# Two attention layers, twice over, on one core: values gathered through HBM, the normaliser broadcast by DMA, and a step list that sets four engines' order

## The chip, the cores and the metric

The kernel runs on one core of a Trainium2 chip. The metric is device time in microseconds (us), the median of several runs. TensorE is called PE, VectorE DVE, ScalarE ACT, GpSimd POOL, and SyncE, whose queue issues most DMAs, SP.

## The reference, cut to what matters

There are 2048 tokens of width 512, 32 heads of 16. Two kinds of layer alternate, A B A B, each on the layer norm of x and added to x:

```
# A: linear attention; pq = q @ w_phi, pk = k @ w_phi, per head
phi = concat(softmax(p), softmax(-p))            # 32 features
kv = phi_k^T v (16 columns); z = sum over tokens of phi_k
o = (phi_q @ kv) / (phi_q . z + 1e-6);  x += o @ wo
# B: each token attends to itself and the tokens 2, 4, ... 14 before it
logits[w] = q . k[s - 2w] / 4 (w = 0..7), masked where s < 2w
o = sum over w of softmax(logits)[w] * v[s - 2w];  x += o @ wo
```

All arrays are bf16. In A, `kv` and `z` sum over all tokens, so every block of tokens of an A layer must be through its keys before any block can go on. In B a block needs only the last 14 tokens of the block before it.

## The kernel before, in words

Tokens are worked in 4 blocks (b = 0 to 3) of 512. L is 0 or 1, the first or second pair of layers. Each block goes through these stages, generator functions in the code:

- `g_ln_first` (layer norm of the input) and, later, the end of `g_out`: ACT and DVE make `rstd`, DVE writes the normalised `xn` (L184), SP transposes it by DMA into `xnT` (L187).
- `g_fold`: at the start w_phi is multiplied into the q and k weights (`WA`), through `wraw`, the loaded raw weights, and `wT`.
- `g_a1`: keys and values of A (L263, L271), exponentials `Ek` on ACT, the softmax sums and scaling on DVE (L282 to L290), and the products summed into three PSUM banks (L296).
- `g_a2`: queries of A (L311), `Eq` on ACT, sums `rS` (L322).
- `g_akv`: once all four blocks are summed, the state goes to SBUF as `ZM` and `R` (L341, L348). This is the barrier of an A layer.
- `g_a3`: denominators (L359), the normaliser `rho` (L374) with time and head on partitions; PE spreads `rho` over the 128 feature rows by 32 matmuls with the 0/1 matrix `indB` (L381) and DVE multiplies that PSUM result into `Eq`, 8 times 128x512 (L386).
- `g_a4`: L397, then `g_out`: 16 matmuls with the output weights (L222), DVE adds to x and sums the rows (L228; L225 in the last layer), one `nmean` (L237), squares on ACT (L242).
- `g_b1`: q, k, v of B, 48 matmuls (L417) and 12 copies by ACT (L419). `QT`, and `KV[0]`, `KV[1]` with 16 columns of the block before (L421). Partition p holds head and one of four parts of the head's 16 dimensions; the 4 column groups c hold the rest.
- `g_b2`: four times, one DVE product `prod` of q with the 8 shifted keys, 128x4096 (L438), and 8 matmuls that sum the dimensions, each with a 128x32 stationary matrix in one of four column positions of the array (L443). Softmax on ACT (L449 to L461) and DVE gives `PT`, whose partitions hold offset and head. Eight DMAs copy it to `Pbc` (L472), where each partition has the weights of its head for all 8 offsets.
- `g_b3`: four times, one DVE product `pav` of `Pbc` with the 8 shifted values (L485), and 8 matmuls with the 128x128 identity that add the offsets (L489); ACT copies to `oT` (L491). Then `g_out`.

`load_B` loads the B weights (`wbraw`, L153; `WoB`, L159) and has POOL reorder them into `WB`; `weight_bound` and `flag` check a bound on the data (a slower path would run otherwise; it does not).

The order of PE, DVE and ACT is that in which the program issues its instructions. `run` gives each generator a start time and conditions, each `yield` returns a number of us, and `drain` always advances the generator with the least time. SP and POOL are not in `_ORDERED`, so their order is the scheduler's. Each engine takes its instructions strictly in its order. Tiles come from rings: 6 buffers of 8 KB a partition (`big`: `Ek`, `prod`, `pav`, `Pbc`), 18 of 4 KB (`med`), 7 of `t2`, 8 PSUM banks.

Of the kernel before, what the change touches and what calls it, by code (L numbers as in the profile page):

```python
# [16 lines left out]
P = 128  # L17
# [12 lines left out]
KVW = 16 + TB  # L30
COLN2_MAX = 3.0
# [4 lines left out]
_ORDERED = {mybir.EngineType.PE, mybir.EngineType.DVE, mybir.EngineType.Activation}  # L36


class _Fast:

    def __init__(self, ctx, tc, A_x, A_wqkv, A_w_phi, A_wo, B_wqkv, B_wo, out):
        self.tc, self.nc = tc, tc.nc
        self.out = out
        e = ctx.enter_context
        self.const = e(tc.tile_pool(name="const", bufs=1))
        self.bigp = e(tc.tile_pool(name="bigp", bufs=6))
        self.medp = e(tc.tile_pool(name="medp", bufs=18))
        self.t2p = e(tc.tile_pool(name="t2p", bufs=7))
        self.small = e(tc.tile_pool(name="small", bufs=2))
        self.psp = e(tc.tile_pool(name="psp", bufs=8, space=PSUM))  # L50
        self.A_x, self.A_wqkv, self.A_w_phi, self.A_wo = A_x, A_wqkv, A_w_phi, A_wo
        self.B_wqkv, self.B_wo = B_wqkv, B_wo

# [11 lines left out]


    def constants(self):
        nc, const = self.nc, self.const
        nc.scalar.preload_act_table_set("natural_log_exp_and_others")
# [9 lines left out]
        with nc.allow_low_precision(reason="0/1 masks"):  # L79
# [5 lines left out]
            maskQ = const.tile([P, H], BF16, name="maskQ")  # L85
            nc.vector.tensor_reduce(out=maskQ[:], in_=ident[:].rearrange("p (h k) -> p h k", k=4),
                                    axis=AX.X, op=ALU.add)
            mask32 = const.tile([P, H], BF16, name="mask32")
            nc.vector.tensor_reduce(out=mask32[:], in_=ident[:].rearrange("p (k h) -> p h k", h=H),
                                    axis=AX.X, op=ALU.add)  # L90
        self.indQK = maskQ
# [24 lines left out]
        nc.gpsimd.memset(self.ones[:], 1.0)  # L116


    def setup(self):
        nc, const = self.nc, self.const  # L120
        self.WA = const.tile([P, NB, 3 * D], BF16, name="WA")
# [20 lines left out]
        PHI = self.t2([NB, DH, 8], "PHI")  # L142
        nc.vector.tensor_tensor(
            out=PHI[:], in0=phis[:].unsqueeze(3).to_broadcast([P, NB, DH, 8]),
            in1=self.maskH[:].unsqueeze(1).unsqueeze(1).to_broadcast([P, NB, DH, 8]), op=ALU.mult)
        self.PHI, self.wraw = PHI, wraw

    def load_B(self):
        nc = self.nc
        wbraw = [self.med([NB, D], "wbraw%d" % i) for i in range(3)]  # L150
        wbv = self.B_wqkv.rearrange("(m p) c -> p m c", p=P)
        for i in range(3):
            nc.sync.dma_start(out=wbraw[i][:], in_=wbv[:, :, i * D:(i + 1) * D])  # L153
        wo_v = self.B_wo.rearrange("(h c dl) n -> dl h c n", c=NB, dl=4)
        for dl in range(4):
            d0 = self.WoB[dl:dl + 1, :, :]
            ps_ = self.WoB[:].ap[0][0]
            dst = bass.AP(d0.tensor, d0.offset, [[4 * ps_, H], [D, NB], [1, D]])
            nc.sync.dma_start(out=dst, in_=wo_v[dl])  # L159
        for i in range(3):  # L160
            for m in range(NB):
                nc.gpsimd.tensor_copy(
                    out=self.WB[:, m, i, :, :].rearrange("p c (h dl) -> p c h dl", dl=4),
                    in_=wbraw[i][:, m, :].rearrange("p (h c dl) -> p c h dl", c=NB, dl=4))

    def weight_bound(self):
        nc = self.nc
        for qk in range(2):
            sq = self.med([NB, D], "sq")
            w = self.WA[:, :, qk * D:(qk + 1) * D]  # L170
            nc.gpsimd.tensor_tensor(out=sq[:], in0=w, in1=w, op=ALU.mult)
            pn = self.ps()
            for m in range(NB):
                nc.tensor.matmul(pn[:], lhsT=self.ones[:], rhs=sq[:, m, :], start=(m == 0), stop=(m == NB - 1))
            okm = self.t2([D], "okm")
            nc.vector.tensor_scalar(out=okm[:], in0=pn[:], scalar1=COLN2_MAX, scalar2=None,
                                    op0=ALU.is_le, op1=ALU.add, accum_out=self.okc[:, qk:qk + 1])


    def ln_apply(self, key, b, mean, rstd, op0):  # L180
        nc = self.nc
        xn = self.med([4, D], "xn")
        for t in range(4):
            nc.vector.tensor_scalar(out=xn[:, t, :], in0=self.x[b][:, t, :], scalar1=mean[:, t:t + 1],  # L184
                                    scalar2=rstd[:, t:t + 1], op0=op0, op1=ALU.mult)
        xnT = self.med([4, NB, P], "xnT")
        nc.sync.dma_start_transpose(out=xnT[:].rearrange("k t c p -> k (t c) p"),  # L187
                                    in_=xn[:].rearrange("p t d -> p (t d)"))
        self.xnT[key, b] = xnT

    def rstd_of(self, var, scale):
        nc = self.nc
        lnv = self.small.tile([P, 4], F32, name="lnv", tag="lnv")
        nc.scalar.activation(out=lnv[:], in_=var, func=ACT.Ln, bias=self.eps_t[:, 0:1], scale=scale)
        rstd = self.small.tile([P, 4], F32, name="rstd", tag="rstd")
        nc.scalar.activation(out=rstd[:], in_=lnv[:], func=ACT.Exp, scale=-0.5)
        return rstd

    def g_ln_first(self, b):
        nc = self.nc  # L200
        stat = self.small.tile([P, 4, 6], F32, name="stat", tag="stat")
        mv = self.small.tile([P, 4, 2], F32, name="mv", tag="mv")
        mean = self.small.tile([P, 4], F32, name="mean", tag="mean")
        for t in range(4):
            nc.vector.bn_stats(out=stat[:, t, :], in_=self.x[b][:, t, :])
            nc.vector.bn_aggr(out=mv[:, t, :], in_=stat[:, t, :])
            if t == 1:
                yield 2.0
        nc.vector.tensor_copy(out=mean[:], in_=mv[:, :, 0])
        rstd = self.rstd_of(mv[:, :, 1], 1.0)  # L210
        yield 2.0
        self.ln_apply("A0", b, mean, rstd, ALU.subtract)

    def g_out(self, key, b, Wo, last, dt):
        nc = self.nc
        xb = self.x[b]
        oT = self.oT[key, b]
        sums = None if last else self.small.tile([P, 4], F32, name="sums", tag="sums")
        for t in range(4):
            y = self.ps()  # L220
            for c in range(NB):
                nc.tensor.matmul(y[:], lhsT=oT[:, c, t * P:(t + 1) * P], rhs=Wo[:, c, :],  # L222
                                 start=(c == 0), stop=(c == NB - 1))
            if last:
                nc.vector.scalar_tensor_tensor(out=xb[:, t, :], in0=y[:], scalar=1.0, in1=xb[:, t, :],  # L225
                                               op0=ALU.mult, op1=ALU.add)
            else:
                nc.vector.scalar_tensor_tensor(out=xb[:, t, :], in0=y[:], scalar=1.0, in1=xb[:, t, :],  # L228
                                               op0=ALU.mult, op1=ALU.add, accum_out=sums[:, t:t + 1])
            if t < 3:  # L230
                yield dt
        if last:
            ov = self.out.rearrange("b (j p) d -> p (b j) d", p=P)
            nc.sync.dma_start(out=ov[:, 4 * b:4 * b + 4, :], in_=xb[:])
            return
        nmean = self.small.tile([P, 4], F32, name="nmean", tag="nmean")
        nc.vector.tensor_scalar(out=nmean[:], in0=sums[:], scalar1=-1.0 / D, scalar2=None, op0=ALU.mult)  # L237
        yield 0.8
        ss = self.small.tile([P, 4], F32, name="ss", tag="ss")
        sqd = self.t2([D], "sqd")  # L240
        for t in range(4):
            nc.scalar.activation(out=sqd[:], in_=xb[:, t, :], func=ACT.Square, bias=nmean[:, t:t + 1],  # L242
                                 accum_out=ss[:, t:t + 1])
        rstd = self.rstd_of(ss[:], 1.0 / D)
        yield 3.5
        self.ln_apply(key, b, nmean, rstd, ALU.add)
# [984 lines left out]
```

## Time and profile before

| | |
|---|---|
| median of 3 runs (lowest, highest) | 517.25 us (516.18, 518.67) |
| the profiled execution | 517.38 us, span 515.6 us |
| PE busy | 401.8 us, 78% |
| DVE busy | 326.1 us, 63% |
| ACT busy | 262.7 us, 51% |
| granted TensorE clock, mean | 0.892 |
| moved by DMA | 25.70 MB |

The span runs from the first to the last instruction of the profiled execution; the run's own time is 1.8 us longer. Busy time of PE counts overlapping matmuls once.

### The profile page before, as it was taken

What the parts mean: (1) busy time and instruction counts of PE and PEld (TensorE: products, weight loads), DVE (VectorE), ACT (ScalarE), POOL (GpSimd) and SP (SyncE); (2) the same over time, 40 slices, a digit from 0 to 9 for tenths busy, and PEclk for the clock granted to TensorE, in tenths of its full rate; (3) what the DMA queues carried; (4) which work ended last, traced back from release to release, by engine and by line L of the source; (5) the groups of instructions that cost most, each with busy time, mean ns of one, the idle gap of its engine ahead of it and who ended that gap; (6) DMA issues with size and microseconds to landing.
All of it is one profiled execution on the core that took longest, in us unless ns stands there. A gap on an engine that the chain in (4) does not pass through costs nothing.

```text
span 515.6 us, 6841 instructions
## 1 busy us (share of the span) xinstructions
PE 401.8 (78%) x2713; PEld 180.2 (35%) x2713; DVE 326.1 (63%) x482; ACT 262.7 (51%) x559; POOL 22.0 (4%) x40
## 2 busy tenths in 40 slices
PE   2769789469967899699689679665896699996493
PEld 1435444224412343244234335422342234342141
DVE  6972234664694896839757524346469389698683
ACT  2566568144844663665546478425374556361210
POOL 2004900000000000000000000000000000000000
PEclk9888889778979899899799969868896879999987
DMA  8726000002202530320320040000131053040402
GB/s 273 178 41 165 0 1 0 3 0 42 42 4 38 123 74 9 69 54 2 61 62 1 0 83 1 0 1 10 32 43 30 12 122 74 9 120 18 108 1 88
DMA packets 51559, 25.70 MB, mean 50 GB/s; under 512 B 35136, under 2 KB 51520, under 8 KB 51520
## 3 DMA queue, kind: packets, MB, share of 16 engines
q1 hardware_dynamic: 49936, 24.12, 20.4%
q10 hardware_dynamic: 1584, 1.07, 0.7%
q8 instruction: 23, 0.38, 0.3%
q14 instruction: 16, 0.13, 0.1%
HBM read 6.31 MB, written 2.10 MB: 16 GB/s over the span
## 4 chain that ended last, share of the span: by engine, by line
PE 53%; DVE 26%; ACT 10%; DMA 5%; issue 3%; SPq 2%; DVEq 0%; ACTq 0%
PE ps L417 14%; PE ps L489 8%; PE ps L222 7%; PE ps L263 5%; DVE Eq L386 5%; DVE prod L438 5%; PE ps L271 5%; ACT sqd L242 4%; PE ps L296 4%; DVE Ek L290 4%; PE ps L311 3%; DVE x L228 3%; PE ps L397 3%; DVE pav L485 3%; DMA xnT<-xn 2%
## 5 line engine op out<-in xcount | busy, mean ns | idle before, releaser
L417 PE MATMUL ps<-xnT,WB 128*128 128x512 bf16 x384 | 101.3, 400 | 3.2 <-DMA xnT<-xn 2.7
L485 DVE TENSOR_TENSOR pav<-Pbc,KV 128x4096 bf16<-128x4096 bf16 x32 | 72.3, 2287 | 10.6 <-DMA Pbc<-PT 10.2
L489 PE MATMUL ps<-pav,ident 128*128 128x512 bf16 x256 | 64.8, 401 | 10.2 <-DVE pav L485 10.2
L438 DVE TENSOR_TENSOR prod<-QT,KV 128x4096 bf16<-128x4096 bf16 x32 | 72.7, 2286 | 0.0
L228 DVE SCALAR_TENSOR_TENSOR x<-ps,x 128x512 bf16<-128x512 f32 x48 | 32.7, 689 | 52.6 <-PE ps L222 52.6
L417 PEld LDWEIGHTS <-WB 128*128 128x128 bf16 x384 | 36.6, 101 | 57.3 <-issue 18.9
L419 ACT CAST KV<-ps 128x512 bf16<-128x512 f32 x64 | 37.0, 593 | 24.2 <-PE ps L417 24.2
L242 ACT ACTIVATE sqd<-x,nmean 128x512 bf16<-128x512 bf16 x48 | 34.7, 722 | 28.5 <-DVE nmean L237 27.4
L491 ACT CAST oT<-ps 128x512 bf16<-128x512 f32 x32 | 18.8, 586 | 48.0 <-PE ps L489 48.0
L263 PE MATMUL ps<-WA,xnT 128*128 128x512 bf16 x128 | 36.9, 435 | 8.0 <-DMA xnT<-xn 8.0
L489 PEld LDWEIGHTS <-ident 128*128 128x128 bf16 x256 | 26.1, 103 | 46.5 <-issue 17.3
L397 PE MATMUL ps<-Eq,R 128*128 128x512 bf16 x64 | 25.4, 535 | 21.4 <-DVE Eq L386 20.2
L386 DVE TENSOR_TENSOR Eq<-ps,Eq 128x512 bf16<-128x512 f32 x64 | 39.4, 683 | 1.8 <-PE ps L381 1.6
L315 ACT ACTIVATE Eq<-ps 128x512 bf16<-128x512 f32 x64 | 34.6, 594 | 8.2 <-PE ps L311 8.2
L282 DVE TENSOR_TENSOR s<-Ek 128x2048 bf16<-128x2048 bf16 x8 | 9.8, 1226 | 43.9 <-ACT Ek L266 43.9
L419 ACT CAST QT<-ps 128x512 bf16<-128x512 f32 x32 | 18.5, 585 | 35.2 <-PE ps L417 35.2
L222 PEld LDWEIGHTS <-oT 128*128 128x128 bf16 x256 | 24.5, 100 | 33.6 <-issue 5.8
L222 PE MATMUL ps<-WoA,oT 128*128 128x512 bf16 x128 | 33.9, 396 | 0.1
L311 PE MATMUL ps<-xnT,WA 128*128 128x512 bf16 x128 | 32.0, 379 | 0.0
L271 PE MATMUL ps<-WA,xnT 128*128 128x512 bf16 x128 | 31.7, 379 | 0.0
L222 PE MATMUL ps<-WoB,oT 128*128 128x512 bf16 x128 | 31.6, 379 | 0.0
L290 DVE TENSOR_TENSOR Ek<-Ek,rk 128x4096 bf16<-128x4096 bf16 x8 | 18.6, 2327 | 19.3 <-ACT rk L288 19.3
(102 smaller groups left out, 436.8 us busy)
## 6 DMA issues: line engine op xcount, KB each, us to landing
Pbc<-PT SPq DMA_DIRECT2D x64, 128.0 KB, 2.7
x<-in_A_x_dram SPq DMA_DIRECT2D x4, 512.0 KB, 9.7
out_dram<-x SPq DMA_DIRECT2D x4, 512.0 KB, 3.0
wbraw<-in_B_wqkv_dram SPq DMA_DIRECT2D x3, 512.0 KB, 5.6
wraw<-in_A_wqkv_dram SPq DMA_DIRECT2D x1, 512.0 KB, 4.3
WA<-in_A_wqkv_dram ACTq DMA_DIRECT2D x1, 512.0 KB, 7.5
wraw<-in_A_wqkv_dram ACTq DMA_DIRECT2D x1, 512.0 KB, 10.0
WoA<-in_A_wo_dram SPq DMA_DIRECT2D x1, 512.0 KB, 10.4
```

Source lines behind the costliest of these rows:

```text
L222: nc.tensor.matmul(y[:], lhsT=oT[:, c, t * P:(t + 1) * P], rhs=Wo[:, c, :], start=(c == 0), stop=(c == NB - 1))
L228: nc.vector.scalar_tensor_tensor(out=xb[:, t, :], in0=y[:], scalar=1.0, in1=xb[:, t, :], op0=ALU.mult, op1=ALU.add, accum_out=sums[:, t:t ...
L242: nc.scalar.activation(out=sqd[:], in_=xb[:, t, :], func=ACT.Square, bias=nmean[:, t:t + 1], accum_out=ss[:, t:t + 1])
L263: nc.tensor.matmul(pk[:], lhsT=xnT[:, t, k, :], rhs=WA[:, k, D:2 * D], start=(k == 0), stop=(k == NB - 1))
L271: nc.tensor.matmul(pv[:], lhsT=xnT[:, t, k, :], rhs=WA[:, k, 2 * D:3 * D], start=(k == 0), stop=(k == NB - 1))
L311: nc.tensor.matmul(pq[:], lhsT=WA[:, k, hb * P:(hb + 1) * P], rhs=xnT[:, :, k, :], start=(k == 0), stop=(k == NB - 1))
L386: nc.vector.tensor_tensor(out=ev, in0=pb[t][:].rearrange("p (a i) -> p a i", a=NB), in1=ev, op=ALU.mult)
L417: nc.tensor.matmul(pp[:], lhsT=WB[:, k, i, c, :], rhs=xnT[:, :, k, :], start=(k == 0), stop=(k == NB - 1))
L419: nc.scalar.copy(out=QT[:, c, :] if i == 0 else KV[i - 1][:, c, 16:KVW], in_=pp[:])
L438: nc.vector.tensor_tensor(out=prod[:], in0=QT[:, c:c + 1, :].to_broadcast([P, NW, TB]), in1=self.win(KV, 0, c), op=ALU.mult)
L485: nc.vector.tensor_tensor(out=pav[:], in0=Pbc[:], in1=self.win(KV, 1, c), op=ALU.mult)
L489: nc.tensor.matmul(po[:], lhsT=self.ident[:], rhs=pavs[c - 1][:, w, :], start=(w == 0), stop=(w == NW - 1))
```

## The change

It rewrites the stages as lists of steps (`step(stage, engine, function)`), and a table of 1387 entries says which step is issued next. The table now sets SP's order too. What the steps do is mostly what they did. These parts differ:

- **Values of B.** `KV[1]` goes. ACT writes `V`, SP writes it to HBM (`VD`, rows of 16 + 2048 tokens, the first 16 zero), and eight DMAs read it back as two `Vg` tiles per block, with key offset and head on the partitions and the 16 dimensions of the head one after the other along the row. Partition group g of four holds the values shifted by 2g tokens, and a window 8 tokens further along the same rows gives the other four offsets. `Pbc` and its 64 DMAs go: `pav` multiplies `PT` itself, broadcast along the dimension, with `Vg`.
- **Sum over offsets.** Eight matmuls per `pav` with the 128x32 matrix `indAV` in four column positions, in place of eight with the 128x128 identity.
- **Normaliser of A.** For blocks 1, 2 and 3, `rho` is written to HBM (`RD`) and read back spread over 128 partitions (`Prho`), in two halves; DVE multiplies each half in one 128x2048 operation. Block 0 keeps the matmuls.
- **Layer norm.** `nmean` is made per 128 tokens: four DVE operations of 128x1 for one of 128x4.
- **Loads.** The loads of the B weights stand ahead of the first transposes. `WoB` has another row order. The output is stored in halves.
- **Buffers.** `big` 8, `med` 16, `t2` 6.
- **Order.** `a2` of blocks 1 and 2 of the first pair, and the weight bound, stand behind the first barrier instead of ahead of it.

The diff, cut to its core (line numbers named in the prediction for the changed kernel are its own):

```diff
-_ORDERED = {mybir.EngineType.PE, mybir.EngineType.DVE, mybir.EngineType.Activation}
+_OPT = {"rho_dma": (1, 2, 3), "pe_resid": {}}
+_ORDERED = {_E.PE, _E.DVE, _E.Activation, _E.SP}
+_ORDER = """
+i i i f i c i g i 0 c i 3 i f e i 3 3 h f j j 3 j f f 3 h 0 f j 4 0 j h j 3 3 j 3 j 3 0 j 5 j 0 1 6 j 0 j 0 0
...
-        self.bigp = e(tc.tile_pool(name="bigp", bufs=6))
-        self.medp = e(tc.tile_pool(name="medp", bufs=18))
-        self.t2p = e(tc.tile_pool(name="t2p", bufs=7))
+        self.bigp = e(tc.tile_pool(name="bigp", bufs=8))
+        self.medp = e(tc.tile_pool(name="medp", bufs=16))
+        self.t2p = e(tc.tile_pool(name="t2p", bufs=6))
...
+        def mean(t):
...
+            nc.vector.tensor_scalar(out=T["nm"][:, t:t + 1], in0=T["sums"][:, t:t + 1], scalar1=-1.0 / D,
+                                    scalar2=None, op0=ALU.mult)
...
+        def wr(s):
...
+            a = rd[0:1, s, 0:1, :]
+            dst = bass.AP(a.tensor, a.offset, [[P, 16], [2 * 16 * P, 8], [1, P]])
+            nc.sync.dma_start(out=dst, in_=T["rho"][:, s, :])
+        def rdb(s):
...
+            src = bass.AP(a.tensor, a.offset, [[0, 16], [2 * 16 * P, 8], [1, 16 * P]])
+            nc.sync.dma_start(out=pr[:].rearrange("p t a i -> p (t a i)"), in_=src)
+        def muld(s):
+            ev = self.Eq[L, b][s]
+            nc.vector.tensor_tensor(out=ev[:], in0=ev[:], in1=T["P", s][:], op=ALU.mult)
...
-        Pbc = self.big([NW, TB], "Pbc")
...
-                nc.sync.dma_start(out=Pbc[:, hf * 4 + g, :], in_=src)
...
+        def vwr():
+            nc.sync.dma_start(out=vd[:, :, 16 + b * TB:16 + (b + 1) * TB], in_=T["V"][:])
+        def vrd(hd, g):
...
+            v0 = vd[0:1, 0:1, b * TB + 2:b * TB + 3]
+            src = bass.AP(v0.tensor, v0.offset + 2 * g + hd * 8 * ROW, [[16 * ROW, H], [ROW, 8], [1, VGW]])
+            nc.sync.dma_start(out=self.Vg[L, b][hd][32 * g:32 * g + 32, :, :], in_=src)
...
-                nc.vector.tensor_tensor(out=pav[:], in0=Pbc[:], in1=self.win(KV, 1, c), op=ALU.mult)
...
-                    nc.tensor.matmul(po[:], lhsT=self.ident[:], rhs=pavs[c - 1][:, w, :],
-                                     start=(w == 0), stop=(w == NW - 1))
...
+        def pav(q):
...
+            a = Vg[q // 2][:, (q % 2) * 4:(q % 2) * 4 + 4, 0:TB]
+            vw = bass.AP(a.tensor, a.offset, [list(a.ap[0]), list(a.ap[1]), [8, 2], [1, TB]])
+            nc.vector.tensor_tensor(out=pv[:], in0=PT[:].unsqueeze(1).to_broadcast([P, NB, 2, TB]), in1=vw,
+                                    op=ALU.mult)
+        def mo(q):
...
+            for hf in range(2):
+                for c in range(NB):
+                    nc.tensor.matmul(po[32 * c:32 * c + 32, :], lhsT=self.indAV[:], rhs=T["p", q][:, c, hf, :],
+                                     start=(hf == 0), stop=(hf == 1), tile_position=(0, 32 * c))
...
-        self.drain()
+        for w in _ORDER.split():
+            key = self.names[int(w, 36)]
+            i = n.get(key, 0)
+            n[key] = i + 1
+            self.threads[key][i]()
```

More of the change, by code (lines that the diff above doesn't have):

```diff
@@ L293, in g_a1, with kv @@
+        def kv(t):
+            if L not in self.kvp:
+                self.kvp[L] = [self.ps() for _ in range(3)]
             for s in range(2):
@@ L337, in bank, with z @@
             return n, self.kvp[L][i][:, 0:n * (P + 1)].rearrange("p (r c) -> p r c", c=P + 1)
[L339 removed]
+        def z(i):
             n, kv = bank(i)
```

888 lines of the change are left out of this document (520 added, 368 removed).

## Prediction

> **What bounds the kernel now.** I read the page's head and chain first, then busy time by stretches cut at the two barriers.
>
> ```profile
> span 515.6 us, 6841 instructions
> PE 401.8 (78%) x2713; PEld 180.2 (35%) x2713; DVE 326.1 (63%) x482; ACT 262.7 (51%) x559; POOL 22.0 (4%) x40
> PE 53%; DVE 26%; ACT 10%; DMA 5%; issue 3%; SPq 2%; DVEq 0%; ACTq 0%
> ```
>
> PE holds over half of the chain, yet is idle for 113.8 us; no engine is full. The tile view of `ZM` gives the barriers: it is first written at 92.8 us and last at 332.9. In the stretches the columns are the stretch, its length, then busy us (instructions) of PE, PEld, DVE, ACT, POOL, then the granted clock, DMA share, GB/s.
>
> ```profile
> L341 DVE TENSOR_TENSOR ZM<-ps,maskR x6: 175/182/184, 92.8 to 332.9; 128x24 bf16<-128x24 f32 x4, 128x16 bf16<-128x16 f32 x2
> 0.00:92.80 92.80, 68.83 (x518) 39.38 (x519) 47.30 (x97) 54.28 (x111) 21.02 (x34) 0.91 0.34 91
> 92.80:332.90 240.10, 194.62 (x1329) 85.23 (x1327) 152.62 (x219) 135.50 (x292) 0.98 (x6) 0.89 0.17 36
> 332.90:515.60 182.70, 138.39 (x874) 55.54 (x873) 126.22 (x167) 72.89 (x156) 0.00 (x0) 0.88 0.21 47
> 0.00:19.70 19.70, 6.75 (x60) 5.88 (x61) 14.70 (x46) 5.40 (x10) 2.87 (x17) 0.97 0.91 267
> 92.80:121.80 29.00, 17.11 (x202) 7.43 (x200) 17.60 (x42) 9.87 (x22) 0.00 (x0) 0.71 0.10 19
> 290.00:300.00 10.00, 1.96 (x9) 0.63 (x8) 3.38 (x11) 6.87 (x18) 0.00 (x0) 0.75 0.28 52
> 332.90:363.50 30.60, 16.04 (x197) 7.10 (x196) 18.64 (x44) 9.59 (x22) 0.00 (x0) 0.77 0.10 18
> 363.50:475.00 111.50, 98.22 (x574) 38.47 (x578) 82.94 (x99) 55.93 (x119) 0.00 (x0) 0.91 0.23 48
> 475.00:515.60 40.60, 24.13 (x107) 9.97 (x99) 24.64 (x25) 7.37 (x15) 0.00 (x0) 0.89 0.23 67
> ```
>
> The first two parts go by PE (68.8 of 92.8 us, 194.6 of 240.1). The last is mixed: after each barrier both PE and DVE wait (16.0 and 18.6 busy of 30.6), in the middle PE is full (98.2 of 111.5), at the end neither is (24 of 41). So I sum the three parts separately, by PE twice and then by the engine that becomes the fuller one.
>
> **Part by part.** The rows that price the edits, from the groups by line (busy us, mean ns | idle before):
>
> ```profile
> L489 PE MATMUL ps<-pav,ident 128*128 128x512 bf16 x256 | 64.8, 401 | 10.2 <-DVE pav L485 10.2
> L443 PE MATMUL ps<-prod,maskQ 128*32 128x512 bf16 x256 | 20.5, 399 | 4.8 <-DVE prod L438 4.8
> L381 PE MATMUL ps<-rho,indB 32*128 32x128 bf16 x256 | 7.8, 228 | 10.2 <-DVE rho L374 7.3 <-DVE Eq L386 2.7 <-DVE x L228 0.2
> L386 DVE TENSOR_TENSOR Eq<-ps,Eq 128x512 bf16<-128x512 f32 x64 | 39.4, 683 | 1.8 <-PE ps L381 1.6
> L282 DVE TENSOR_TENSOR s<-Ek 128x2048 bf16<-128x2048 bf16 x8 | 9.8, 1226 | 43.9 <-ACT Ek L266 43.9
> L485 DVE TENSOR_TENSOR pav<-Pbc,KV 128x4096 bf16<-128x4096 bf16 x32 | 72.3, 2287 | 10.6 <-DMA Pbc<-PT 10.2 <-issue 0.4
> L237 DVE TENSOR_SCALAR nmean<-sums 128x4 f32<-128x4 f32 x12 | 2.0, 171 | 0.4
> L421 DVE COPY KV<-KV 128x64 bf16<-128x64 bf16 x12 | 2.1, 176 | 0.0
> L311 PE MATMUL ps<-xnT,WA 128*128 128x512 bf16 x128 | 32.0, 379 | 0.0
> L322 PE MATMUL ps<-Eq,indS 128*32 128x128 bf16 x256 | 7.5, 228 | 8.1 <-ACT Eq L315 7.7
> L174 PE MATMUL ps<-sq,ones 128*128 128x512 bf16 x8 | 1.9, 379 | 0.0
> ```
>
> *Sum over offsets.* The new 256 matmuls have the form, count and column positions of L443: 20.5 us for L489's 64.8, so PE loses 44.3 us, 22.15 in each of the last two parts. (The Trainium skill, TensorEngine Tiling (Array Packing), Theoretical Speedup and Key Properties, states up to 4x for four column tiles, but that a change of tiling mode drains the array. By 4x alone the new matmuls would take 16.2 us and the total would be 4 us lower; L443 shows 3.2x, the shortfall in line with such a drain, so the row stands.)
>
> *Normaliser.* Three blocks of four lose L381 (7.8 x 3/4 = 5.9 us of PE) and L386 (39.4 x 3/4 = 29.6 us of DVE). They gain 12 products of 128x2048, priced by L282 at 1.23 us: 14.7. DVE gains 14.8 us, 7.4 a half.
>
> *Products of B.* `pav` keeps its elements and types; I keep 2287 ns. *Small ones.* 36 more `nmean` at 0.17 cost DVE 6.1 us, 4.1 and 2.1 by halves; half of L421 goes, 0.5 us each. ACT's 262.7 us do not change.
>
> *What is moved out of the first part.* `a2` of two blocks (32.0/8 + 7.5/8 = 4.94 us of PE each) and L174 (1.9): 11.8 us of PE pass behind the barrier. ACT at the first barrier, before:
>
> ```order
> L327 ACTIVATE rS<-ps 128x256
> L328 ACTIVATE rS<-rS 128x256
> L370 ACTIVATE Ds<-Ds,deneps_t 128x128
> L371 ACTIVATE Ds<-Ds 128x128
> L399 CAST oT<-ps 128x512 x4
> ```
>
> and now, where L589 and L590 are those denominators and L512 the exponentials of `a2`:
>
> ```order
> L589 ACTIVATE Ds_963<-Ds_963,deneps_t_99 128x128
> L590 ACTIVATE Ds_963<-Ds_963 128x128
> L589 ACTIVATE Ds_974<-Ds_974,deneps_t_99 128x128
> L590 ACTIVATE Ds_974<-Ds_974 128x128
> L512 ACTIVATE Eq_987<-ps_967 128x4x128
> L512 ACTIVATE Eq_988<-ps_967 128x4x128
> L512 ACTIVATE Eq_987<-ps_980 128x4x128
> L512 ACTIVATE Eq_988<-ps_980 128x4x128
> L512 ACTIVATE Eq_987<-ps_992 128x4x128
> ```
>
> Two blocks' denominators stand together now, and projections fill the time in which PE waited for DVE's products.
>
> *The start.* SP before, and now below it:
>
> ```order
> L138 DMA x_86<-in_A_x_dram 128x4x512
> L139 DMA WoA<-in_A_wo_dram 128x4x512
> L159 DMA WoB<-in_B_wo_dram 32x4x512 x4
> L187 DMA_TRANSPOSE xnT<-xn 128x16x128 x4
> L153 DMA wbraw_674<-in_B_wqkv_dram 128x4x512
> ```
>
> ```order
> L206 DMA x_89<-in_A_x_dram 128x4x512
> L207 DMA WoA<-in_A_wo_dram 128x4x512
> L257 DMA wbraw<-in_B_wqkv_dram 128x4x512 x3
> L266 DMA WoB<-in_B_wo_dram 32x2048 x4
> L269 DMA vd_146<-zpad 512x1x16
> L322 DMA_TRANSPOSE xnT<-xn 128x16x128 x4
> ```
>
> Three loads of 512 KB have passed ahead of the transposes, for whose results the first projections wait.
>
> ```profile
> wbraw<-in_B_wqkv_dram SPq DMA_DIRECT2D x3, 512.0 KB, 5.6
> 19.74 1.91 PE L263 MATMUL ps<-WA,xnT 128*128 128x512 bf16 x4
> ```
>
> 1.57 MB at the 267 GB/s of the first 19.7 us are 5.9 us, so projections start at 25.6, not 19.7. Bounds: 0 (if the queue has room) and 9 (half of three loads at 5.6 us each).
>
> *First part:* 68.8 - 6.75 = 62.1 us of PE lay behind 19.7, less 11.8 is 50.3. Idle there was 11.0; I keep 7. 25.6 + 50.3 + 7 = **83** (79 to 89).
>
> *Second part:* 194.6 - 22.15 - 2.9 + 11.8 = 181.3 us of PE. Of its idle 45.5 us, the moved `a2` fills about 10 of the 11.9 behind the barrier and 5 of the 10.2 behind `Pbc` go. In 290:300, where PE waited for the last block's layer norm, most of 8.0 goes: keys, values and sums of other blocks now stand there. That leaves 22; I take 20. **201** (189 to 221). DVE's 152.6 - 7.4 + 4.1 - 0.5 = 148.8 and ACT's 145.8 fit under it. (The Trainium skill, TensorE: Matmul & The Clock Gate, Part 1, states that PE's clock halves after an idle window of about 3.4 us and recovers after a busy one. The 0.71 granted in 92.8:121.8 agrees. If the filled gap brought full clock there, 17.1 x 0.29 = 5 us more would go, which the sum above does not take.)
>
> *Third part:* PE falls to 138.4 - 22.15 - 2.9 = 113.3, DVE to 126.2 - 7.4 + 2.1 - 0.5 = 120.4: DVE becomes the fuller engine. It was idle 12.0 us after the barrier, 28.6 in the middle, 16.0 at the end. After the barrier the DMA path adds a write and a read, partly beside block 0's matmuls: 15 (12 to 24). In the middle PE no longer holds it: 9 (4 to 18). At the end the wait for `Pbc` (4.9 us of 10.2) goes and a shorter sum follows: 8. 120.4 + 15 + 9 + 8 = **152** (140 to 172).
>
> *The gather.* DVE's b2 and b3 of the first pair, before:
>
> ```order
> L465 TENSOR_TENSOR PT_1815<-E_1784,rden_1799 128x1024
> L421 COPY KV_1582<-KV_1331 128x4x16
> L438 TENSOR_TENSOR prod_1853<-QT_1580,KV_1581 128x4096
> L438 TENSOR_TENSOR prod_1870<-QT_1580,KV_1581 128x4096
> L438 TENSOR_TENSOR prod_1886<-QT_1580,KV_1581 128x4096
> L438 TENSOR_TENSOR prod_1908<-QT_1580,KV_1581 128x4096
> L485 TENSOR_TENSOR pav_1936<-Pbc_1817,KV_1331 128x4096
> ```
>
> and now:
>
> ```order
> L769 TENSOR_TENSOR PT_1948<-E_1838,rden_1934 128x1024
> L794 TENSOR_TENSOR pav_1950<-PT_1948,Vg_1773 128x4096
> L794 TENSOR_TENSOR pav_1964<-PT_1948,Vg_1773 128x4096
> L794 TENSOR_TENSOR pav_1978<-PT_1948,Vg_1804 128x4096
> L794 TENSOR_TENSOR pav_1998<-PT_1948,Vg_1804 128x4096
> ```
>
> Before, another block's four products had to hide the copy of `PT`; now `pav` follows `PT` at once, and what it needs from DMA depends on the value projection alone. But that is more:
>
> ```profile
> Pbc<-PT SPq DMA_DIRECT2D x64, 128.0 KB, 2.7
> out_dram<-x SPq DMA_DIRECT2D x4, 512.0 KB, 3.0
> WoB<-in_B_wo_dram SPq DMA_DIRECT2D x4, 128.0 KB, 7.5
> 170.00:180.00 10.00, 10.00 (x53) 3.82 (x52) 8.80 (x8) 6.10 (x11) 0.17 (x1) 0.90 0.72 159
> ```
>
> A gather is 32 x 8 x 520 x 2 B = 266 KB, eight a block 2.13 MB, four blocks 8.5 MB in each half. At the 267 GB/s of the start's loads that is 8 us a block, at the 159 GB/s of a burst of `Pbc` 13; the write of V, priced by the output's 512 KB, 3.0. Eight `prod` of two blocks (8 x 2.29 = 18 us) stand ahead of the first `pav`, and one block's `pav` (9) ahead of the next's, so I cost the gathers at nothing; without that cover a block would pay 11 to 16 us.
>
> *SP's written order.* Twice as many bytes now share one queue whose order nobody else mends: in the second part 16 gathers stand ahead of the transpose of the last block to leave A, and in the third the stores, which wait for DVE, stand among the last 16 gathers.
>
> ```profile
> L472 SPq DMA_DIRECT2D Pbc<-PT x64: 543/604/994, 172.6 to 485.0; - x64
> DMA to landing us min/median/max: 4.2/4.3/6.2
> ```
>
> The trace has no gather. By a `Pbc` issue (0.6 us) 16 take 10 us; by a gather's bytes at 159 GB/s, 27. The transpose (4.3 us to landing, second row) is then late by up to that, and behind it stand that block's q, k and v. PE has other blocks' projections and sums meanwhile; I take 0 and let the upper bounds of the second and third part carry 10 each.
>
> **Sum.** 83 + 201 + 152 = 436 us of span, plus 1.8 (517.38 less 515.6) = **438**. The median of 517.25 is within 0.2 of the profiled execution, so the sum is compared with it directly.
>
> **The rivals.** *Only the work goes.* The new order merely moves the waits: PE's 401.8 - 44.3 - 5.9 = 351.6, the old idle 113.8 less the 10.2 behind `Pbc`, plus 5.9 at the start: 461, run **463**. For it: waits for PE by DVE and ACT are spread over many groups. Against: 20 us of the idle time lie in two stretches (92.8:121.8 and 290:300) that get other work. 0.18.
>
> *Nearly gapless.* The low ends, 79 + 189 + 140 + 1.8 = **410**. For it: 363.5:475 shows PE 88% busy already. Against: barrier and layer norm chains stay. 0.15.
>
> *Slower: the gather sets the pace.* From barrier to V's write 50 us (30.6 and 20 of projections), then 8.5 MB at r, then a block's products and the end, 20: 70 + 8500/r. At the 70 GB/s of four `WoB` loads in flight (0.52 MB in 7.5 us) the last part takes 191 and the second some 243: 83 + 243 + 191 + 1.8 = **519**. It decides below 70 GB/s; the burst rows show twice that. 0.05.
>
> That the column tiles do not overlap, so that the change does not do what it says, L443 excludes.
>
> **The numbers.** The forecast, 420 to 455, has 0.60; the remaining 0.02 is a tie. I predict 438. The range 404 to 466 takes in the forecast, most of the next two cases, and leaves the slower one out. A measurement of this kernel can tell about 0.5% from no change: faster 0.93, same 0.02, slower 0.05.
>
> **What would show it.** Right: the group of `indAV` near 20 us; `Eq` by `Prho` near 1.23 us each; the barrier at 79 to 89 and the second 189 to 221 later; no wait of `pav` for `Vg` over a few us; DVE fuller than PE in the last part. Wrong: `pav` waiting for `Vg` by the ten us, `Eq` for `Prho` beyond 15 us after a barrier, or SP holding transposes behind gathers.

## The result and the profile after

The changed kernel takes **424.23 us** (median of 4 runs, 423.0 to 424.97); the kernel before, beside it, 516.81 (516.18 to 518.67). The ratio is 0.820, 95% interval 0.817 to 0.823: 18% faster, and 14 us below the 438 forecast. The profiled run took 424.97, of which 422.1 is span; the 2.9 around it were 1.8 before.

The busy times of the page, and its chain:

```profile
PE 327.1 (78%) x2499; PEld 147.4 (35%) x2521; DVE 317.0 (75%) x476; ACT 253.6 (60%) x559; POOL 18.1 (4%) x39
PE 41%; DMA 24%; DVE 19%; ACT 10%; issue 2%; SPq 1%; ACTq 0%; DVEq 0%
```

PE is as full as before in share (78%), DVE is nearly as full (75%, from 63%), and waits for DMA hold 24% of the chain, up from 5%. The tile view of `ZM` and the busy time between the barriers (columns as before):

```profile
L547 DVE TENSOR_TENSOR ZM<-ps,maskR x6: 175/183/184, 74.5 to 268.0; 128x24 bf16<-128x24 f32 x4, 128x16 bf16<-128x16 f32 x2
0.00:74.50 74.50, 50.24 (x378) 29.11 (x383) 48.85 (x93) 42.72 (x89) 17.11 (x33) 0.93 0.47 114
74.50:268.00 193.50, 167.34 (x1357) 75.40 (x1369) 148.70 (x226) 139.97 (x314) 0.83 (x5) 0.94 0.48 95
268.00:422.10 154.10, 109.51 (x772) 42.87 (x777) 119.44 (x158) 70.92 (x156) 0.15 (x1) 0.85 0.54 119
74.50:114.00 39.50, 35.87 (x398) 16.98 (x398) 30.21 (x83) 32.17 (x78) 0.15 (x1) 1.00 0.45 98
```

The parts take 74.5, 193.5 and 154.1 us, for 92.8, 240.1 and 182.7 before and 83, 201 and 152 forecast. The stretch behind the first barrier (last row) is the plainest sign of the new order: PE was busy 17 of 29 us there, at a granted clock of 0.71; now it is busy 36 of 39.5, at 1.00.

The groups that answer to the rows that priced the edits:

```profile
L801 PE MATMUL ps<-pav,indAV 128*32 128x512 bf16 x256 | 22.6, 449 | 23.9 <-DVE pav L794 23.5 <-ACT oT L807 0.3
L627 DVE TENSOR_TENSOR Eq<-Eq,Prho 128x2048 bf16<-128x2048 bf16 x12 | 14.6, 1222 | 11.2 <-DMA Prho<-rd 11.2
L794 DVE TENSOR_TENSOR pav<-PT,Vg 128x4096 bf16<-128x4096 bf16 x32 | 71.9, 2287 | 17.7 <-DMA Vg<-vd 8.9 <-PE ps L801 8.6
L382 DVE TENSOR_SCALAR nmean<-sums 128x1 f32<-128x1 f32 x48 | 7.2, 153 | 1.4
L676 PE MATMUL ps<-xnT,WB 128*128 128x512 bf16 x384 | 87.6, 384 | 4.2 <-DMA xnT<-xn 4.1
```

Every edited operation costs what its nearest row said, within about 2 us in each group. The projections of B (L676) were not edited and still show 87.6 us of busy time, for 101.3 before; this comes up again below. The idle times behind the bar have changed: `pav` waits 17.7 us (10.6 before), `Eq` 11.2 for `Prho`, and PE waits longer for the transposed input `xnT`. The page's rows of that wait are below, the changed kernel's and then those of the kernel before, with the landing of the transposes after the change:

```profile
L506 PE MATMUL ps<-xnT,WA 128*128 128x512 bf16 x128 | 31.9, 400 | 13.8 <-DMA xnT<-xn 13.2
L435 PE MATMUL ps<-WA,xnT 128*128 128x512 bf16 x123 | 30.4, 391 | 9.8 <-DMA xnT<-xn 9.4
DMA to landing us min/median/max: 4.2/4.7/10.0
```

```profile
L263 PE MATMUL ps<-WA,xnT 128*128 128x512 bf16 x128 | 36.9, 435 | 8.0 <-DMA xnT<-xn 8.0
L417 PE MATMUL ps<-xnT,WB 128*128 128x512 bf16 x384 | 101.3, 400 | 3.2 <-DMA xnT<-xn 2.7
```

With the 4.1 of L676 that is 26.7 us for 10.7. Of the 26.7, 9.4 lie at the start and 17.3 in the second part, where the kernel before waited 8.0 in one place. The 13.2 are one wait, at 185 to 198 us: 14 gathers are issued from 176 to 187, and the transpose behind them, of the first block to leave B, takes 10.0 us to land. The 7.3 us that `pav` waits for sums in the second part lie there too, since PE, which makes the sums, stands at that transpose.

The DMA issues of the page, with the median from issue to landing at the end of a row:

```profile
Vg<-vd SPq DMA_DIRECT2D x64, 260.0 KB, 8.1
vd<-V SPq DMA_DIRECT2D x8, 512.0 KB, 3.3
```

### The profile page after: what moved, and what is told of

Read it like the earlier page. It is cut to its first block, busy times and chain, and to the rows that moved or that the text cites. A ratio compares the mean times of both kernels' runs of the same rounds, so it can differ in the third digit from the quotient of the medians.

```text
span 422.1 us, 6496 instructions
## 1 busy us (share of the span) xinstructions
PE 327.1 (78%) x2499; PEld 147.4 (35%) x2521; DVE 317.0 (75%) x476; ACT 253.6 (60%) x559; POOL 18.1 (4%) x39
## 4 chain that ended last, share of the span: by engine, by line
PE 41%; DMA 24%; DVE 19%; ACT 10%; issue 2%; SPq 1%; ACTq 0%; DVEq 0%
PE ps L676 16%; DMA xnT<-xn 5%; PE ps L506 5%; PE ps L363 5%; PE ps L423 4%; DMA vd<-V 4%; DMA Prho<-rd 4%; DMA Vg<-vd 3%; DMA rd<-rho 3%; DVE x L376 3%; PE ps L478 3%; DVE xn L317 3%; ACT Eq L512 2%; DMA wraw<-in_A_wqkv_dram 2%; PE ps L435 2%
## 5 line engine op out<-in xcount | busy, mean ns | idle before, releaser
L676 PE MATMUL ps<-xnT,WB 128*128 128x512 bf16 x384 | 87.6, 384 | 4.2 <-DMA xnT<-xn 4.1
L794 DVE TENSOR_TENSOR pav<-PT,Vg 128x4096 bf16<-128x4096 bf16 x32 | 71.9, 2287 | 17.7 <-DMA Vg<-vd 8.9
L734 DVE TENSOR_TENSOR prod<-QT,K 128x4096 bf16<-128x4096 bf16 x32 | 71.4, 2285 | 3.1 <-ACT QT L690 1.6
L676 PEld LDWEIGHTS <-WB 128*128 128x128 bf16 x384 | 37.0, 99 | 53.6 <-issue 10.5
L376 DVE SCALAR_TENSOR_TENSOR x<-ps,x 128x512 bf16<-128x512 f32 x64 | 42.9, 684 | 10.6 <-PE ps L363 10.5
L506 PE MATMUL ps<-xnT,WA 128*128 128x512 bf16 x128 | 31.9, 400 | 13.8 <-DMA xnT<-xn 13.2
L807 ACT CAST oT<-ps 128x512 bf16<-128x512 f32 x32 | 18.4, 590 | 40.2 <-PE ps L801 40.2
L512 ACT ACTIVATE Eq<-ps 128x512 bf16<-128x512 f32 x64 | 34.0, 625 | 13.4 <-PE ps L506 13.4
L801 PE MATMUL ps<-pav,indAV 128*32 128x512 bf16 x256 | 22.6, 449 | 23.9 <-DVE pav L794 23.5
L435 PE MATMUL ps<-WA,xnT 128*128 128x512 bf16 x123 | 30.4, 391 | 9.8 <-DMA xnT<-xn 9.4
L429 ACT ACTIVATE Ek<-ps 128x512 bf16<-128x512 f32 x64 | 32.9, 636 | 2.6 <-PE ps L423 2.6
L363 PE MATMUL ps<-WoB,oT 128*128 128x512 bf16 x124 | 32.6, 408 | 1.1 <-ACT oT L807 0.8
L423 PE MATMUL ps<-WA,xnT 128*128 128x512 bf16 x122 | 29.0, 379 | 0.7 <-DVE WA L241 0.4
L690 ACT CAST QT<-ps 128x512 bf16<-128x512 f32 x32 | 18.7, 586 | 13.4 <-PE ps L676 13.4
L658 ACT CAST oT<-ps 128x512 bf16<-128x512 f32 x32 | 16.8, 597 | 14.1 <-PE ps L652 14.1
L506 PEld LDWEIGHTS <-WA 128*128 128x128 bf16 x128 | 12.8, 102 | 30.9 <-DMA xnT<-xn 13.8
L627 DVE TENSOR_TENSOR Eq<-Eq,Prho 128x2048 bf16<-128x2048 bf16 x12 | 14.6, 1222 | 11.2 <-DMA Prho<-rd 11.2
```

Source lines behind the costliest of these rows:

```text
L376: nc.vector.scalar_tensor_tensor(out=xb[:, t, :], in0=T[t][:], scalar=1.0, in1=xb[:, t, :], op0=ALU.mult, op1=ALU.add, **kw)
L423: nc.tensor.matmul(pk[:], lhsT=xnT[:, t, k, :], rhs=self.WA[:, k, D:2 * D], start=(k == 0), stop=(k == NB - 1))
L429: nc.scalar.activation(out=T["E"][:, t, s, :], in_=T["k", t][:], func=ACT.Exp, scale=1.0 - 2.0 * s)
L435: nc.tensor.matmul(pv[:], lhsT=xnT[:, t, k, :], rhs=self.WA[:, k, 2 * D:3 * D], start=(k == 0), stop=(k == NB - 1))
L506: nc.tensor.matmul(pq[:], lhsT=self.WA[:, k, hb * P:(hb + 1) * P], rhs=xnT[:, :, k, :], start=(k == 0), stop=(k == NB - 1))
L512: nc.scalar.activation(out=self.Eq[L, b][s][:, :, hb, :], in_=T[hb][:].rearrange("p (t i) -> p t i", t=4), func=ACT.Exp, scale=1.0 - 2.0 * s)
```

## The experiments

My theory from the two traces: (a) the operations take off what the rows say, but most of the gain comes from the list that fills PE's gaps; (b) what is left is held by transfers, for the bytes of the gathers delay the transposes in the second part and the last products in the third. The rivals: the operations alone do it; the gathers are hidden as forecast; the start is held by the loads ahead of the transposes. All times below are medians of four runs unless said otherwise, beside 424.2.

**The operations without the list.** The kernel before with the new operations, its planner and the order of its loads kept. Its gathers stand where the copies of `PT` stood, behind the softmax.

```diff
-                nc.vector.tensor_tensor(out=pav[:], in0=Pbc[:], in1=self.win(KV, 1, c), op=ALU.mult)
...
+                nc.vector.tensor_tensor(out=pav[:], in0=PT[:].unsqueeze(1).to_broadcast([P, NB, 2, TB]), in1=vw,
+                                        op=ALU.mult)
...
+                for hf in range(2):
+                    for k in range(NB):
+                        nc.tensor.matmul(po[32 * k:32 * k + 32, :], lhsT=self.indAV[:], rhs=pavs[c - 1][:, k, hf, :],
```

> The kernel before with the new operations (V written and gathered through HBM, column-tiled sums, the normaliser of blocks 1 to 3 by DMA, the new WoB layout, buffers 8/16/6) but with the old planner and its start times; loads and nmean as before. Theory, operations and order each carry a part: 450 to 475 us, PE busy near 352 us, PE idle still over 100 us. Rival one, the operations carry it all: 424 to 435 us. Rival two, the list alone carries it: over 500 us.

Measured **494.58 us**, ratio 0.954 (0.948 to 0.961). Its stretches, and its 384 projections of B:

```profile
0.00:93.60 93.60, 68.62 (x512) 39.27 (x520) 47.35 (x98) 54.53 (x111) 20.87 (x34) 0.91 0.35 91
93.60:323.80 230.20, 175.67 (x1219) 70.95 (x1233) 145.32 (x198) 133.73 (x292) 0.83 (x5) 0.87 0.38 80
323.80:493.50 169.70, 116.08 (x769) 42.31 (x777) 118.64 (x146) 71.95 (x156) 0.00 (x0) 0.85 0.50 108
L441 PE MATMUL ps<-xnT,WB 128*128 128x512 bf16 x384 | 103.3, 406 | 0.6 <-DMA xnT<-xn 0.6
L422 PE MATMUL ps<-Eq,R 128*128 128x512 bf16 x64 | 24.5, 510 | 32.6 <-DVE Eq L399 24.5 <-DVE Eq L411 8.1
```

That is between the 450 to 475 of the theory and the second rival's 500. The operations alone give 4.6 of the 18.0 per cent; the list, with the loads and the split mean that go with it, gives the other 13.4 on top of them. The list with the old operations was not run, so the split holds in this order alone. PE loses 41 us of busy time (401.8 to 68.6 + 175.7 + 116.1 = 360.4), but the run only 23, since PE now waits longer elsewhere (32.6 us for `Eq` in front of L422, where the same products, L397, waited 21.4 before). The sum is also a warning about busy time: the same matmuls as in the changed kernel are busy 360.4 us here and 327.1 there.

**The sum over offsets undone, one pair at a time.** Each `pav` is summed by eight matmuls of full width, the selector padded with zeros, for the eight that share the columns.

```diff
+                        nc.tensor.matmul(po[:], lhsT=self.indW[:, (3 - c) * H:(7 - c) * H], rhs=T["p", q][:, c, hf, :],
+                                         start=(hf == 0 and c == 0), stop=(hf == 1 and c == NB - 1))
```

In the first pair:

> The changed kernel, but in the first pair of layers the sum over offsets is made by eight full 128x128 matmuls with zero-padded matrices instead of four column positions: 22 us more PE work between the barriers, same result. Theory, PE bounds the second part (167 of 193.5 us busy): 439 to 446 us. Rival, PE's idle time there absorbs it: 424 to 431 us.

In the second pair:

> The same in the second pair of layers alone: 22 us more PE work behind the second barrier. Theory, DVE and the gathers set the last part (PE 109.5 of 154.1 us busy): 427 to 436 us, under half of the added work. Rival, PE is on the path there too: 442 to 447 us.

Measured **433.73** and **428.61 us**. The part that the edit touches, of each:

```profile
75.20:277.80 202.60, 185.83 (x1354) 85.73 (x1368) 149.22 (x226) 140.90 (x314) 0.83 (x5) 0.97 0.45 91
```

```profile
268.00:426.50 158.50, 126.41 (x770) 53.42 (x777) 119.55 (x158) 71.08 (x156) 0.15 (x1) 0.91 0.53 116
```

PE takes 18.5 and 16.9 us more; the time rises by 9.5 and 4.4. So a microsecond of PE's busy time counts for half a microsecond in the second part and for a quarter in the third. The first is below what I expected of a part that goes by PE, and above the rival; the second is as expected.

**The queries' scores back ahead of the barrier.** ACT's order at the barrier shows the move (L512 to L527 are the two blocks' exponentials and sums; those rows go up, past the denominators L589):

```diff
+L512 ACTIVATE Eq<-ps 128x4x128 x10
+L526 ACTIVATE rS<-ps 128x256
+L527 ACTIVATE rS<-rS 128x256
...
 L589 ACTIVATE Ds<-Ds,deneps_t 128x128
 L590 ACTIVATE Ds<-Ds 128x128
-L512 ACTIVATE Eq<-ps 128x4x128 x10
-L526 ACTIVATE rS<-ps 128x256
-L527 ACTIVATE rS<-rS 128x256
```

> The queries' softmax and sums of blocks 1 and 2 of the first pair go back ahead of the first barrier, as the kernel before had them; the rest of the list as it is. Theory of the prediction: they are 9.9 us of TensorE that fill waits behind the barrier, so the barrier comes 8 to 11 us later (82 to 86) while the second part loses less than 4: 429 to 435 us. Rival: the second part is nearly gapless by now (167 of 193 us), so that work taken out of it shortens it by as much: 422 to 427, barrier still 82 to 86.

Measured **434.41 us**, 10.2 more, as the theory had it:

```profile
0.00:84.70 84.70, 61.03 (x478) 34.23 (x479) 48.13 (x93) 51.99 (x109) 17.07 (x33) 1.00 0.41 101
84.70:278.10 193.40, 162.73 (x1274) 72.64 (x1275) 148.54 (x226) 130.94 (x294) 0.83 (x5) 0.91 0.46 95
84.70:124.00 39.30, 30.84 (x303) 14.00 (x301) 29.86 (x83) 22.66 (x57) 0.15 (x1) 0.87 0.41 99
```

The barrier comes 10.2 us later and the second part is as long as before (193.4 for 193.5), with less in it. Behind the barrier the work costs nothing; ahead of it, all of its price (9.9 us by the rows of the kernel before). This one move of the list is worth 10 us.

**The bytes of the gathers.** First half of them, so that half of the value columns are left out of the result:

```diff
-            src = bass.AP(v0.tensor, v0.offset + 2 * g + hd * 8 * ROW, [[16 * ROW, H], [ROW, 8], [1, VGW]])
-            nc.sync.dma_start(out=self.Vg[L, b][hd][32 * g:32 * g + 32, :, :], in_=src)
+            src = bass.AP(v0.tensor, v0.offset + 2 * g + hd * 8 * ROW, [[16 * ROW, H], [ROW, 4], [1, VGW]])
+            nc.sync.dma_start(out=self.Vg[L, b][hd][32 * g:32 * g + 32, 0:4, :], in_=src)
...
-            a = Vg[q // 2][:, (q % 2) * 4:(q % 2) * 4 + 4, 0:TB]
+            a = Vg[q // 2][:, 0:4, 0:TB]
```

> Each gather brings only the first four of the eight value rows of a tile (133 KB for 266), in both layers, and both products of a tile multiply the same four rows; half of the value columns are left out of the result. Number of gathers, of landings that are waited for, and of products stay. Theory: the bytes ahead of them on the queue hold the value write, the transposes and the last gathers, so with half the bytes the third part (154.1 us) falls by 6 to 15 and the second (193.5) by 2 to 10: 400 to 416 us, and the write of V lands in 5 us or less at the end. Rival 1: the count of transfers in flight holds them, not bytes: 421 to 425, V write still 8 us or more. Rival 2: the second part has no slack in DMA's favour, the third alone moves: 409 to 419.

Measured **400.78 us** (399.81 to 401.2), 23.4 less. Its parts, then the rows of PE's wait for `xnT`, of the products and of the gathers:

```profile
74.60:255.20 180.60, 169.27 (x1369) 75.39 (x1370) 148.05 (x226) 139.90 (x314) 0.83 (x5) 0.96 0.35 78
255.20:398.30 143.10, 108.67 (x777) 42.74 (x777) 118.91 (x158) 70.75 (x156) 0.15 (x1) 0.87 0.39 99
L506 PE MATMUL ps<-xnT,WA 128*128 128x512 bf16 x128 | 32.4, 405 | 3.8 <-DMA xnT<-xn 3.3
L794 DVE TENSOR_TENSOR pav<-PT,Vg 128x4096 bf16<-128x4096 bf16 x32 | 71.6, 2284 | 0.2
Vg<-vd SPq DMA_DIRECT2D x64, 130.0 KB, 3.4
```

The second part is 12.9 us shorter, more than the 2 to 10 expected, the third 11.0. The two gains show in different waits. In the second, PE's busy time is up by 1.9, so its idle time falls by 14.8; and its wait for transposes there falls by 14.0, from 17.3 to the 3.3 of L506 (L435 at the start still waits 9.0). In the third, `pav` waited 8.9 us for `Vg` and 1.2 for sums, and does so no more (0.2 in the whole run). The landing of a gather falls from 8.1 to 3.4 us for half the size, and the longest landing of a write of V from 9.5 to 6.0, where I had expected 5 or less at the end. As many transfers as before are in the queue, so their number is not what holds it. Half the rows are half the packets too: which of the two, bytes or packets, sets the price stays open.

Then twice of them, in the second pair:

```diff
-            nc.sync.dma_start(out=self.Vg[L, b][hd][32 * g:32 * g + 32, :, :], in_=src)
+            for _ in range(2 if L == 1 else 1):
+                nc.sync.dma_start(out=self.Vg[L, b][hd][32 * g:32 * g + 32, :, :], in_=src)
```

> The changed kernel with each of the 32 gathers of the second pair issued twice, the same bytes to the same place: 8.5 MB more behind the second barrier, 39 us at the 220 GB/s of its fullest slices. Theory, the transfers at the end are on the path: 444 to 465 us. Rival, the gathers are hidden beside DVE's products as I forecast: 424 to 432 us.

Measured **523.16 us** (10 runs), ratio 1.009 (1.006 to 1.012): more than either theory. SP's waits (us in all, times, the longest) and the last part say why:

```profile
SPq L711 <- DMA Vg<-vd: 120.1, 44, 3.7
268.80:521.00 252.20, 115.80 (x772) 43.65 (x777) 119.71 (x158) 71.19 (x156) 0.15 (x1) 0.72 0.44 107
```

The second copy goes to the place of the first, and SP waits for gathers to land 44 times, 120.1 us in all; in the changed kernel it does so 19 times, 16.0 us in all. So this run does not raise the traffic (107 GB/s in the last part, less than the 119 of the changed kernel) but makes it serial, and it is no measure of bytes. It shows something else: with each gather made twice, one behind the other, the last part takes 252 us, and the whole gain is gone.

**The normaliser by matmuls again, in the second pair.**

```diff
-                self.s_a3(L, b, b in _OPT["rho_dma"])
+                self.s_a3(L, b, L == 0 and b in _OPT["rho_dma"])
```

The list behind the second barrier is written anew for these steps, block after block.

> The changed kernel, but behind the second barrier all four blocks' normaliser is spread by matmuls and multiplied from PSUM, block after block; the first pair keeps the DMA. Adds 7.4 us to DVE and 3 us to PE, takes away the write and read (1.9, 4.5, 6.3 and 4.6 us on the chain at 271 to 295). Theory, after a barrier the DMA path costs more in latency than it saves in work: 414 to 422 us, PE busy sooner behind the barrier. Rival, DVE is the fuller engine there and the 7.4 us count: 428 to 433 us.

Measured **425.82 us** (425.35 to 426.96), 1.6 more: neither. Behind the second barrier the chain of the changed kernel, then of this one (start, length, what):

```profile
273.68 4.47 DMA rd<-rho
278.16 6.25 DMA Prho<-rd
```

```profile
278.23 4.80 DVE Eq L607 x8
284.68 4.87 DVE Eq L607 x8
```

A write of 4.5 us and a read of 6.3 stand in the place of rounds of eight DVE products, 4.8 and 4.9 us each. The DMA path saves DVE's work but is as long a path: in this place the normaliser by DMA is a draw, 0.4% ahead.

**The start.** Once with the two halves of the weight fold in the other order (a few entries of the list), once with B's loads behind the four transposes on SP:

```diff
 L207 DMA WoA<-in_A_wo_dram 128x4x512
+L322 DMA_TRANSPOSE xnT<-xn 128x16x128 x4
 L257 DMA wbraw<-in_B_wqkv_dram 128x4x512 x3
 L266 DMA WoB<-in_B_wo_dram 32x2048 x4
...
-L322 DMA_TRANSPOSE xnT<-xn 128x16x128 x4
```

> The changed kernel with the two weight folds exchanged in the list, so that the half of the raw weights that lands first (4.3 us) is worked first; nothing else moves. Theory from the trace of the changed kernel, the start is late because DVE's first copy waits for weights that land at 11.9 us and the statistics stand behind it: first projection near 21 instead of 27.0, 417 to 421 us. Rival, the 1.57 MB of loads ahead of the transposes make it late, as I forecast: 423 to 425 us.

> The changed kernel with the loads of the B weights and the reordering by GpSimd moved behind the four first transposes. My forecast's term: first projection 5.9 us sooner, 417 to 420 us. Rival, DVE's wait for the late half of the raw weights sets the start: 422 to 426 us.

Measured **422.69** (421.72 to 424.58) and **424.36 us** (422.5 to 425.36). The chain of the changed kernel opens:

```profile
1.94 9.91 DMA wraw<-in_A_wqkv_dram
12.96 0.69 DVE wT L232
13.65 0.61 DVE stat L340
```

and that of the run with the fold turned round:

```profile
12.12 1.90 PE ps L228 x16
...
14.04 1.94 ACT wT L232 x2
...
17.46 0.20 ACT lnv L310
```

The loads ahead of the transposes cost next to nothing: with them moved behind, the first projection starts at 26.3 us for 27.0, and the run is as long. What holds the start is DVE's order: its copy `wT` of the half of the weights that lands at 11.9 us stands ahead of the statistics of `x`, and the layer norm is late with it. Turned round, DVE copies the half that lands first, the first projection starts at 25.8 us for 27.0, and the barrier comes at 72.9. That is 1.5 us of gain in the median, with ranges that overlap, where I expected 3 to 7: now ScalarE's copies of the late half stand ahead of the layer norm's logarithm, at 17.5 us.

**The end.** Chain of the changed kernel in the last 60 us:

```profile
356.56 8.87 DMA vd<-V
369.77 9.46 DMA vd<-V
...
384.07 8.59 DMA out_dram<-x
392.68 10.13 DMA Vg<-vd
```

The write of V, 3.3 us in the median, takes 8.9 and 9.5 behind gathers; and the last gather is released by the landing of a store. So: V's write from ScalarE's queue; the stores behind all gathers; both, with the fold turned round.

```diff
-            nc.sync.dma_start(out=vd[:, :, 16 + b * TB:16 + (b + 1) * TB], in_=T["V"][:])
+            nc.scalar.dma_start(out=vd[:, :, 16 + b * TB:16 + (b + 1) * TB], in_=T["V"][:])
```

```diff
-L710 DMA Vg<-vd_147 32x8x520 x6
-L394 DMA out_dram<-x_88 128x2x512
-L710 DMA Vg<-vd_147 32x8x520 x2
-L394 DMA out_dram<-x_88 128x2x512
-L710 DMA Vg<-vd_147 32x8x520 x8
+L710 DMA Vg<-vd_147 32x8x520 x16
+L394 DMA out_dram<-x_88 128x2x512 x2
```

> The changed kernel with the eight writes of V issued by ACT on its own DMA queue, right behind V's last copy, instead of by SP; SP no longer waits for V ahead of other blocks' gathers. Theory, the end is set by the chain V write (8.9 and 9.5 us to landing) and gathers behind one another: 412 to 420 us, the gain behind the second barrier. Rival, the bytes of the gathers set it, whoever issues the write: 421 to 425 us.

> The two stores of the third output block go behind all gathers in the queue's order. Theory: in the last 60 us a store that waits for its layer norm held the order, and the gathers behind it; the last gather then lands 3 to 8 us earlier and the run takes 418 to 422 us. Rival: the gathers behind wait for buffers or for DMA anyhow and the stores now end last: 423 to 427.

> Together: the second half of the weight fold first, the write of V from ScalarE's queue, and the stores behind the gathers. Apart the first two gave -1.5 and -2.1 us. Theory: they lie in different parts and add up, with the stores 416 to 420. Rival: the write of V and the stores are the same wait at the end, so only one of them counts: 420 to 423.

Measured **422.15** (421.31 to 423.62), **424.35** (423.04 to 425.94) and **419.97 us** (419.66 to 420.49). Alone, each move leaves the other wait standing, and both times lie where the rival had them. With the write on the other queue:

```profile
357.89 8.56 DMA vd<-V
...
382.58 9.15 DMA out_dram<-x
391.75 9.67 DMA Vg<-vd
```

With all three:

```profile
363.09 5.59 DMA vd<-V
368.70 7.47 DMA Vg<-vd
376.19 11.28 DMA Vg<-vd
387.48 9.17 DMA Vg<-vd
```

A queue of its own does not spare the write its wait among gathers (8.56 us). The stores gain nothing alone: the write's 9.34 us is then in the chain, and the last gather waits for another gather to land instead of a store and starts at 391.7 us for 392.7. With the others the end is gathers behind gathers. The three together are the best full version of the study, 4.3 us or 1% under the changed kernel. That is on the border between theory (416 to 420) and rival (420 to 423), so the run does not decide between them. That what is left there is the traffic is argued from the half gathers, not shown in this version.

## Why the prediction was right, and where its steps failed

The direction and the mechanism held, and the time came out 14 us under the forecast, inside its range. By its own steps:

- *Sum over offsets.* Price right: 22.6 us for the 20.5 from L443. (The rate that the Trainium skill, TensorEngine Tiling (Array Packing), Theoretical Speedup, gives as up to 4x would make it 16.2, an estimate; the ratio here is 64.8 / 22.6 = 2.9.) Its worth was wrong: I took all 22.15 us of each pair off the path in the second part; put back, 18.5 us of PE's busy time cost 9.1 there.
- *Normaliser and small edits.* Right: `Eq` 14.6 for 14.7; `nmean` 7.2 for 2.0 + 6.1. DVE's 148.7 and 119.4 us of the last parts stand for 148.8 and 120.4.
- *The start.* 27.0 for 25.6, and the cause fell: I charged 5.9 us to three loads ahead of the transposes, and moving them away brought the projections 0.7 us forward and the run nothing. (The upper bound, half of three loads at 5.6 us, is 8.4 and not 9.) The weight copy in DVE's order was late, an engine whose order I had not shown at this place.
- *First part, 83 for 74.5.* The failed terms are PE's 50.3 us and the 7 of idle time: from 27.0 us to the barrier PE is busy 45.5 and idle 2. The 11.8 us that I passed behind the barrier hold as far as they were tested: two of the three items, 9.9 us, cost 10.2 of run time when put back. The sums of a third block (32 matmuls of L520) went behind the barrier too, which I had not counted, 0.9 us by the row of L322. Most of the rest is busy time that shrank for the same work: 126 products of `Ek` and `vaug` in this part are busy 7.7 us, 221 ns each, for 11.7 and 267 before.
- *Second part, 201 for 193.5.* Two errors against each other. PE was busy 167.3, not 181.3; idle 26.2, not 20. The first is no work left out: I subtracted busy times as if they were amounts of work. The same 384 projections are busy 103.3 us under the old order and 87.6 under the new, and of my 351.6 us PE showed 360.4 under the old and 327.1 under the new. Matmuls that follow each other closely overlap in the profile, and busy time counts the overlap once: 384 projections of 384 ns each are busy 87.6 us, 228 for each, while one that nothing overlaps counts its whole 379 (the median of one) and up to 631 (the longest). The second error is the term taken as 0, the transposes behind gathers in SP's written order. I had named it and given 10 us of the upper bound to it. The transpose that I named, of the last block to leave A, cost PE 4.1 us; the next one, of the first block to leave B, cost 13.2. With half the gathers these 17.3 are 3.3, and the part is 12.9 us shorter. This sign of being wrong, SP holding transposes behind gathers, came true.
- *Clock.* I left 5 us aside, in case the filled gap brought full clock. The clock did rise behind the barrier: 1.00 for 0.71, as the Trainium skill, TensorE: Matmul & The Clock Gate, Part 1, would have it, and 0.87 when the scores are moved back. What of PE's 14 us less in the second part is clock and what is overlap, no run separates.
- *Third part, 152 for 154.1.* DVE is the fuller engine, as forecast, busy 119.4 us for 120.4. After the barrier it is idle 13.2 us (I took 15; 6.9 of them `rho` waits for a landing of `rd`, 4.0 `Eq` for `Prho`), in the middle 14.9 (9), at the end 6.6 (8). That the sum is so close is partly luck, since the misses go both ways:

```profile
268.00:308.00 40.00, 24.30 (x243) 11.19 (x246) 26.80 (x66) 18.95 (x45) 0.15 (x1) 0.79 0.42 98
308.00:395.00 87.00, 68.15 (x432) 25.97 (x434) 72.14 (x74) 47.97 (x105) 0.00 (x0) 0.88 0.63 132
395.00:422.10 27.10, 17.07 (x103) 5.71 (x97) 20.50 (x20) 4.00 (x7) 0.00 (x0) 0.81 0.45 110
```

- *The gather, costed at nothing.* Failed in the third part: `pav` waits 8.9 us for `Vg` there, more than the few I allowed and close to the ten that I named as a sign of being wrong. With half the gathers the third part takes 143.1. In the second part `pav` does not wait for `Vg`.
- *The rivals.* "Only the work goes" (463) is nearest to what the operations show without the list, and even that was too good for it: 494.6, as longer waits came with the old order. "Nearly gapless" (410) was right on the first part alone, which ended below its 79. "The gather sets the pace" (519) fell. The 523 of the run with doubled gathers lies near it by chance, with parts of 75, 193 and 252 us for the rival's 83, 243 and 191. With transfers side by side, half of the gathered bytes are worth 13 us of the second part and 11 of the third.

## What to carry to other kernels

Price an operation by its row, but an order by its gaps: here the same operations were worth 5% under a planner that did not know them and 18% under a list that filled the waits, and moving 10 us of ready work from ahead of a barrier to behind it gained 10 us. When a load is traded for bigger transfers, look not only at who reads the data but at who queues behind them: here PE lost 17.3 us at transposes behind gathers in the second part, and DVE 8.9 us at the gathers themselves in the third. And do not subtract busy times of TensorE across orders: the same matmuls were busy 360.4 us under one and 327.1 under another, with overlap counted once and the granted clock not the same (0.87 and 0.94 in the second part).

## What the runs showed of the hardware

- A 512 KB write to HBM landed in 3.3 us in the median and in 8.6 to 9.5 behind gathers, the 8.56 from a queue of its own; a transpose in 4.7 and up to 10.0.
- Two transfers to the same tile place ran one after the other: SP waited for gathers 44 times, 120.1 us in all and up to 3.7 each, for 19 times and 16.0 us without the second transfers, and the last part went from 154 to 252 us.
- 256 matmuls in four column tiles showed 22.6 us of PE busy time for the 64.8 of as many full-width ones.
